# Batch 0's k loaded in rows of nine tokens and turned on TensorE, its scores by pairs of heads, decay folded into q, one MLP block's second part spread over output steps, the last output tile in halves

## The chip, the cores and the metric

The kernel runs on one core of a Trainium2 chip. The metric is the device time of one execution in microseconds (us). The core has five engines that run their own instruction lists and wait for each other by semaphores: TensorE (PE, with its weight loads PEld), VectorE (DVE), ScalarE (ACT), GpSimd (POOL) and SyncE (SP). SP, ACT and POOL also issue DMAs. Matrix products land in PSUM, eight banks of 128 x 512 fp32; everything else lies in SBUF.

## The reference

Eight batches of eight heads, 576 tokens, 64 features each. First a retention layer (attention without softmax, with a decay mask), then an MLP whose hidden layer is h times cos(h). The result is 4608 x 512 in fp32.

```python
scores = (q @ k.T) / sqrt(64)
gamma = 1 - 2 ** (-5 - head)
ret = scores * where(i >= j, gamma ** (i - j), 0)
x = (ret @ v)                    # heads side by side: 4608 x 512
h = x @ w_in                     # 512 x 2048
out = (h * cos(h)) @ w_out       # 2048 x 512
```

## The kernel before

**Retention by chunks.** The 576 tokens of a batch are cut into NCH = 5 chunks of 128 (the last 64); NP = 4 is the number of head pairs. The decay gamma^(i-j) is split: v is multiplied by gamma^-j (`vmul`, table WV, on POOL), and the result by gamma^i / 8 (table UP) when it leaves PSUM. For each chunk r of batch b: `scores` multiplies turned k by turned q (64-row operands, two banks, one for each head of a pair), and DVE multiplies both by a triangle (`mask`, tile rt); `rest` adds, into one bank (po), the state of the chunks before times q (weights sb) and the masked scores times v (rt, vb), then adds k times v into the state (bank st), which ACT copies to sb; at its end DVE multiplies po by UP into xt (L476).

**Layouts.** k and q are needed with features on partitions (tile kqt). From batch 2 on `prep` casts k and q on POOL into kqb, multiplies v, and a transposing DMA on SP's queue writes kqt. Batches 0 and 1 are turned on PE: k by `turn_k` (a product with the identity, one chunk at a time, from kqb), q by `turn_q` (from rows of nine tokens, 2304 contiguous bytes for each partition: a pair of heads fills 128 partitions and is turned by 18 small transposes). k and v of a chunk are loaded by `load`, 128 tokens by eight heads, in pieces of 256 bytes. Batch 0's q is loaded by `load_q0` in the nine-token rows and cast on DVE (`cast_q0`, L280).

**MLP by tiles.** The 4608 tokens are cut into NTB = 9 tiles of TB = 512, which straddle the batches. `mlp1(j, dt)` computes step dt of 16: four products (xt, win) into one of four mm banks, cosine on ACT (tile cb, L504), product with h on DVE (tile gt, L507). `mlp2(j, st, part)` adds a quarter of the 16 products that give the 128 output tokens st; after the last part ACT copies the bank to osb (L538), and ACT's queue stores it (L545). `bank` hands out the mm banks in turn and skips the ones that an unfinished output holds. The weights are loaded and cast by POOL's DMAs: `w_in_load` in five pieces (steps 0, 2, 4, 8, 12), `w_out_load` in four.

**Order.** `emit` writes the order out by hand. Each `self.s.op` goes into its engine's list at that place, and waits are derived from the `Buf` objects that it reads and writes. Before the first MLP step stand batch 0's chunks 0 to 3, with `spin` (idle products with the identity) between them; chunk 4 comes between steps 2 and 6 of the first tile (`turn_k`, `scores`, `rest`). Batch 1's first chunks stand between the output steps of tile 0, the others between the first parts (320 of 512 tokens) of tile 1's steps. The second parts (192 tokens) follow in a row, then tile 1's output steps with batch 2's chunks between. From then on each tile's output steps hold the next batch's chunks. On POOL the first w_in piece stands behind the casts of k's chunks 0 to 2 and two multiplications of v; the loads of batch 1 wait on SP for the landing of w_out's first piece.

L401 and L403 are the lines of all matmuls (in `group`: all but the last, and the last), L318 the casts, L308 `vmul`, L267 `load`, L296 `w_in_load`, L303 `w_out_load`, L365 and L381 the evictions of `turn_k` and `turn_q`, L428 `mask`, L471 the copies of the state.

## Time and profile before

| | us |
|---|---|
| median of 3 runs | 316.08 (315.33 to 316.46) |
| profiled execution | 315.09 |
| its span, first to last instruction | 313.3 |
| PE busy | 301.7 |
| PEld busy | 159.8 |
| DVE busy | 174.2 |
| ACT busy | 161.7 |
| POOL busy | 93.2 |

The granted clock of TensorE is 1.000 over the span, and DMA moves 48.85 MB. Matmuls overlap in the pipeline, so that a single one lasts longer (379 ns for 512 columns) than the step from one to the next (0.216 us). Rows of the timeline give the start, the duration, the engine, the line, the operation, output and inputs, and in brackets the idle time before it with what ended that. The matmuls of `spin` count as busy. An engine that is idle costs nothing unless PE waits for it in the end.

### The profile page before, as it was taken

How to read it: one execution, taken by the hardware profiler on the slowest of the kernel's cores; microseconds unless marked ns; L12 is line 12 of the kernel's file. 1: busy time of each engine (PE TensorE's matmuls, PEld its weight loads, DVE VectorE, ACT ScalarE, POOL GpSimd, SP SyncE). 2: the span in 40 equal slices, each digit the busy share in tenths (PEclk: the TensorE clock that was granted, in tenths of full speed). 3: DMA queues.
4: the chain of work that ended last, by engine and by line, in shares of the span. 5: the costliest groups of instructions: out<-in, count | busy, mean ns of one | idle time of the engine just before them, and what ended most of it. 6: DMA issues, size and time to landing. Idle time of an engine off the chain costs nothing.

```text
span 313.3 us, 6427 instructions
## 1 busy us (share of the span) xinstructions
PE 301.7 (96%) x2519; PEld 159.8 (51%) x2552; DVE 174.2 (56%) x301; ACT 161.7 (52%) x290; POOL 93.2 (30%) x128
## 2 busy tenths in 40 slices
PE   7979999999999999999999999999999999999996
PEld 6754455666554455445545554455445554444442
DVE  3567624788427852685458554865577448405700
ACT  7566525784347533762377236723573347317711
POOL 2693027444455434553535434110000000000000
DMA  7999999999999999999999999940001000120021
GB/s 211 214 180 207 200 220 231 260 192 187 233 252 170 239 216 249 224 221 231 233 231 202 237 245 212 137 86 36 33 0 69 36 33 0 51 85 1 15 82 73
DMA packets 142815, 48.85 MB, mean 156 GB/s; under 512 B 132545, under 2 KB 137665, under 8 KB 142785
## 3 DMA queue, kind: packets, MB, share of 16 engines
q1 hardware_dynamic: 132320, 34.22, 61.2%
q0 software_dynamic: 5280, 4.78, 9.4%
q10 hardware_dynamic: 5184, 9.44, 8.7%
q8 instruction: 20, 0.33, 0.5%
q14 instruction: 11, 0.08, 0.1%
HBM read 36.70 MB, written 9.44 MB: 147 GB/s over the span
## 4 chain that ended last, share of the span: by engine, by line
PE 90%; DMA 3%; issue 2%; ACT 2%; DVE 2%; SPq 1%; POOL 1%; DVEq 0%
PE mm L401 60%; PE mm L403 20%; PE po L401 6%; DMA vn<-in_v_dram 3%; PE sc L401 2%; PE st L401 1%; ACT cb L504 1%; DVE rt L428 1%; SPq L276 1%; DVE gt L507 0%; SPq L267 0%; DVE xt L476 0%; ACT osb L538 0%; ACT kqt L365 0%; POOL vb L308 0%
## 5 line engine op out<-in xcount | busy, mean ns | idle before, releaser
L507 DVE TENSOR_TENSOR gt<-mm,cb 128x512 bf16<-128x512 f32 (+2 forms) x160 | 101.2, 637 | 60.7 <-ACT cb L504 58.1
L401 PE MATMUL mm<-xt,win 128*128 128x512 bf16 (+2 forms) x471 | 116.7, 358 | 0.8 <-DVE xt L476 0.3
L504 ACT ACTIVATE cb<-mm,c_pih 128x512 bf16<-128x512 f32 (+2 forms) x160 | 101.9, 645 | 27.6 <-PE mm L403 26.8
L401 PE MATMUL mm<-wout,gt 128*128 128x512 bf16 x408 | 111.7, 379 | 3.2 <-issue 3.0
L401 PEld LDWEIGHTS mm<-xt,win 128*128 128x128 bf16 x480 | 44.6, 98 | 48.5 <-DVE gt L507 1.7
L401 PEld LDWEIGHTS mm<-wout,gt 128*128 128x128 bf16 x432 | 39.3, 98 | 44.4
L538 ACT ACTIVATE osb<-mm 128x512 f32<-128x512 f32 x36 | 21.5, 597 | 71.7 <-PE mm L403 71.7
L403 PE MATMUL mm<-xt,win 128*128 128x512 bf16 (+2 forms) x160 | 57.2, 358 | 0.3
L403 PE MATMUL mm<-wout,gt 128*128 128x512 bf16 x144 | 54.6, 379 | 0.2
L308 POOL TENSOR_TENSOR vb<-vn,wv 128x512 bf16<-128x512 f32 (+1 forms) x40 | 41.7, 1043 | 35.8 <-DMA vn<-in_v_dram 29.6
L476 DVE TENSOR_TENSOR xt<-po,up 128x512 bf16<-128x512 f32 (+1 forms) x39 | 24.7, 634 | 45.7 <-PE po L403 45.7
L471 ACT ACTIVATE sb<-st 64x256 bf16<-64x256 f32 x64 | 24.1, 377 | 35.6 <-PE st L403 34.7
L318 POOL CAST kqb<-kn 128x512 bf16<-128x512 f32 (+1 forms) x40 | 24.4, 611 | 59.1 <-DMA kn<-in_k_dram 51.1
L428 DVE TENSOR_TENSOR rt<-sc,mk 128x512 bf16<-128x512 f32 (+1 forms) x54 | 30.5, 600 | 4.8 <-PE sc L403 4.8
L403 PEld LDWEIGHTS mm<-xt,win 128*128 128x128 bf16 x160 | 15.7, 98 | 15.7
L318 POOL CAST kqb<-qn 128x512 bf16<-128x512 f32 (+1 forms) x30 | 18.4, 615 | 16.1 <-DMA qn<-in_q_dram 16.1
L403 PEld LDWEIGHTS mm<-wout,gt 128*128 128x128 bf16 x144 | 14.1, 98 | 17.0
L428 DVE TENSOR_TENSOR rt<-mm,mk 128x512 bf16<-128x512 f32 x26 | 16.6, 682 | 0.1
L401 PE MATMUL po<-rt,vb 128*64 128x128 bf16 (+1 forms) x273 | 15.2, 220 | 0.0
L401 PEld LDWEIGHTS po<-kqt,sb 128*128 128x128 bf16 x124 | 8.6, 98 | 7.8 <-DVE rt L428 1.5
L401 PEld LDWEIGHTS po<-rt,vb 128*64 128x64 bf16 (+1 forms) x273 | 9.3, 108 | 5.9 <-DVE rt L428 2.1
L401 PE MATMUL po<-kqt,sb 128*128 128x128 bf16 (+1 forms) x124 | 11.2, 213 | 0.5 <-POOL vb L308 0.2
(88 smaller groups left out, 147.5 us busy)
## 6 DMA issues: line engine op xcount, KB each, us to landing
out_dram<-osb ACTq DMA_DIRECT2D x36, 256.0 KB, 3.6
kn<-in_k_dram SPq DMA_DIRECT2D x32, 256.0 KB, 4.6
vn<-in_v_dram SPq DMA_DIRECT2D x32, 256.0 KB, 5.4
qn<-in_q_dram SPq DMA_DIRECT2D x24, 256.0 KB, 4.8
wout<-in_moe_w_out_dram POOLq DMA_DIRECT2D x4, 512.0 KB, 14.0
win<-in_moe_w_in_dram POOLq DMA_DIRECT2D x3, 512.0 KB, 7.5
qn<-in_q_dram SPq DMA_DIRECT2D x4, 288.0 KB, 4.7
kn<-in_k_dram SPq DMA_DIRECT2D x8, 128.0 KB, 3.6
```

The costliest lines, as they stand in the source:

```text
L276: s.dma("sp", f"q0_{c}", lambda e: e.dma_start(dst, src), writes=[self.bQN[c]])
L308: self.s.op(eng, lambda e: e.tensor_tensor(bass.AP(self.VB[i][r], 0, v3), self.staged("v", r, v3[1:]), bass.AP(self.WV, r * H_, [[NCH * H_ ...
L318: self.s.op(eng, lambda e: e.tensor_copy(o, f), reads=[self.bST32[x][r]], writes=[bt[i][r]])
L401: self.nc.tensor.matmul(o, a, b, **kw)
L403: return s.done("pe", self.nc.tensor.matmul(o, a, b, **kw), reads, writes)
L428: self.s.op("dve", lambda e: e.tensor_tensor(bass.AP(self.RT[k][hp], 0, p3), bass.AP(sc[0], 0, p3), bass.AP(self.MK, 0, [[CH, ck], [0, NP] ...
L471: s.op("act", lambda e: e.activation(bass.AP(self.SB[r % 2], 64 * hp * 512 + 64 * hp, [[512, 64], [128, NP], [1, D_]]), bass.AP(self.ST, 6 ...
L476: s.op("dve", lambda e: e.tensor_tensor(bass.AP(self.XT, t0, [[NP * XR, 128], [XR, NP], [1, ck]]), bass.AP(po, 0, [[512, 128], [CH, NP], [ ...
L504: s.op("act", lambda e: e.activation(co, mo, AF.Sin, bias=self.C_PIH.ap(), scale=1.0), reads=[bm, self.bC], writes=[bcb])
L507: s.op("dve", lambda e: e.tensor_tensor(bass.AP(g, dt * TB + o, [[16 * TB, 128], [1, n]]), mo, co, ALU.mult), reads=[bm, bcb], writes=[bg])
L538: s.op("act", lambda e: e.activation(o.ap(), m.ap(), AF.Copy), reads=[bm], writes=[bo])
```

## The change

What it does, in the order of the kernel:

- Batch 0's k is loaded in the nine-token rows, as q is (`load0`, eight loads alternating k and q by head pair), ahead of v's chunks 0 to 3. All eight are cast on POOL (`cast0`); k's rows use a part of the second gt tile that is free then. PE turns both (`turn0`), q's eviction multiplies by the decay, and `back0` turns k back into the token layout (kqb) that the state needs. All 576 tokens of k are turned, so the turning of chunk 4 falls away.
- Batch 0's scores run by pairs of heads over chunks 0 to 3 at once (`scores0`), their masked results lie in the gt tile too. `rest` is cut into `sums` and `state`; batch 0 runs three states, four sums in a row (evicted by ACT and DVE by turns), and the fourth state. There are three sb tiles.
- The factor gamma^i / 8 goes from the result into q: `qmul` on POOL in place of q's cast from batch 2 on (table UPN), and a multiplication by DVE in the evictions of `turn_q` and `turn0`. The result leaves PSUM by a plain copy.
- POOL's list: eight casts, v 0, w_in 0, v 1, v 2, w_in 1, v 3, w_in 2 to 4, w_out. v's chunk 4 and batch 1 are loaded once w_in's last piece has landed. ACT loads its table for the cosine before the turning.
- Chunk 4 of batch 0 goes from the first tile's MLP steps to its output steps 2 and 4; batch 1's first chunks move by a step each, and k's chunk 2 is turned in an mm bank.
- The second parts of tile 1's steps run two by two ahead of output steps 0 to 7 of that tile; batch 2's chunks stand at steps 2, 5, 8, 11 and 14. Each gt step has two `Buf` objects, one for either part, so that the first output tokens wait for the first part only.
- `mlp2` skips the bank that it has just finished when that bank would be next.
- The last 128 output tokens are computed in two halves of 256 columns, the first copied by DVE and stored from SP, the second copied by ACT and stored from ACT (`last`).

```diff
+SP1 = 3 * 64 + CH
...
+    def consts_n(self):
+        s = self.s
+        s.op("act", lambda e: e.activation(self.WV.ap(), self.LW.ap(), AF.Exp, scale=-1.0),
+             reads=[self.bLW], writes=[self.bWV])
+        s.op("act", lambda e: e.activation(self.UPN.ap(), self.LW.ap(), AF.Exp,
+                                           bias=self.C_LN8.ap(), scale=1.0),
+             reads=[self.bLW, self.bC], writes=[self.bUPN])
...
+    def load0(self, x, c):
         n = 9 * D_
-        self.s.op("dve", lambda e: e.tensor_copy(
-            bass.AP(self.QX[0], c * n, [[NP * n, 128], [1, n]]),
-            bass.AP(self.QN, c * n, [[NCH * DM, 128], [1, n]])),
-            reads=[self.bQN[c]] + self.bST32["q"], writes=[self.bQ0[c]])
+        dst = bass.AP(self.XN[x], c * n, [[NCH * DM, 128], [1, n]])
+        src = bass.AP(self.src[x], 2 * c * S_ * D_, [[n, 128], [1, n]])
+        self.s.dma("sp", f"{x}0_{c}", lambda e: e.dma_start(dst, src), writes=[self.bN0[x][c]])
...
+    def cast0(self, x, c):
+        n = 9 * D_
+        more = [] if x == "q" else [b for i in range(2) for b in self.bGT[1][2 * NP + 2 * c + i]]
+        self.s.op("pool", lambda e: e.tensor_copy(
+            self.rows0(x, c, 128, [0, [1, n]]),
+            bass.AP(self.XN[x], c * n, [[NCH * DM, 128], [1, n]])),
+            reads=[self.bN0[x][c]] + self.bST32[x], writes=[self.bX0[x][c]] + more)
...
+    def qmul(self, eng, b, r):
+        i = b % 2
+        self.mul(eng, "q", r, self.KQB[i], 2 * DM * r + DM, NCH * 2 * DM, self.UPN, self.bUPN, self.bQB[i][r])
...
-        for x in "kq":
-            self.cast("pool", x, b, r)
+        self.cast("pool", b, r)
+        self.qmul("pool", b, r)
         self.vmul("pool", b, r)
...
+    def turn9(self, m, rows, reads, bm):
...
         m2 = m.ap().bitcast(BF16)
-        self.group([(m2[64 * hp:64 * hp + 64, 64 * t:64 * t + 64],
-                     bass.AP(self.QX[i], 64 * hp * NP * n + c * n + t * D_, [[NP * n, 64], [1, D_]]),
+        self.group([(m2[64 * hp:64 * hp + 64, 64 * t:64 * t + 64], rows(hp, t),
                      bass.AP(self.ID, 64 * hp * 128 + 64 * hp, [[128, 64], [1, 64]]),
                      dict(start=True, stop=True, is_transpose=True))
...
+    def turn_q(self, b, c, bank):
+        s, i, n = self.s, b % 2, 9 * D_
+        m, bm = bank
...
+        done = s.op("dve", lambda e: e.tensor_tensor(o, f, self.up9(c), ALU.mult),
+                    reads=[bm, self.bUP], writes=[Buf()])
...
+    def turn0(self, x, c, bank, eng):
+        s, (m, bm) = self.s, bank
+        f = self.turn9(m, lambda hp, t: self.rows0(x, c, 64, [t * D_, [1, D_]], hp),
+                       [self.bX0[x][c]], bm)
...
+        if x == "q":
+            fn = lambda e: e.tensor_tensor(o, f, self.up9(c), ALU.mult)
+        elif eng == "dve":
+            fn = lambda e: e.tensor_copy(o, f)
+        else:
+            fn = lambda e: e.activation(o, f, AF.Copy)
+        done = s.op(eng, fn, reads=[bm] + [self.bUP] * (x == "q"), writes=[self.bT0[x][c]])
...
+    def back0(self, c, bank):
+        s, (m, bm) = self.s, bank
+        n = NCH - 1
+        t = self.group([(bass.AP(m, r * CH, [[512, 128], [1, 128]]),
+                         bass.AP(self.KQT[0], c * S_ + r * CH, [[TP, 128], [1, CH]]), self.ID.ap(),
+                         dict(start=r == 0, stop=r == n - 1)) for r in range(n)],
+                       [self.bT0["k"][c], self.bID], [bm])
+        o = bass.AP(self.KQB[0], c * 128, [[NCH * 2 * DM, 128], [2 * DM, n], [1, 128]])
+        f = bass.AP(m, 0, [[512, 128], [CH, n], [1, 128]])
+        done = s.op("act", lambda e: e.activation(o, f, AF.Copy), reads=[bm], writes=[Buf()])
...
+    def scores0(self, c, sc):
+        s, n = self.s, NCH - 1
+        mms = []
+        for r in range(n):
+            for hp in range(2):
+                base = 64 * hp * TP + c * S_ + CH * r
+                mms.append((
+                    bass.AP(sc[hp][0], r * CH, [[512, 128], [1, CH]]),
+                    bass.AP(self.KQT[0], base, [[TP, 64], [1, CH]]),
+                    bass.AP(self.KQT[0], TQ + base, [[TP, 64], [1, CH]]),
+                    dict(start=r == 0, stop=r == n - 1)))
+        t = self.group(mms, [self.bT0["k"][c], self.bT0["q"][c]], [sc[0][1], sc[1][1]])
...
+        for hp in range(2):
+            s.op("dve", lambda e: e.tensor_tensor(
+                bass.AP(self.GT[1], (2 * c + hp) * TB, [[16 * TB, 128], [CH, n], [1, CH]]),
+                bass.AP(sc[hp][0], 0, p3),
+                bass.AP(self.MK, 0, [[CH, 128], [0, n], [1, CH]]), ALU.mult),
+                reads=[sc[hp][1], self.bMK], writes=list(self.bR0[2 * c + hp]))
...
+    def rest(self, b, r, po=None, eng="dve"):
+        done = self.sums(b, r, po, eng)
+        if r < NCH - 1:
+            self.state(b, r)
+        done()
...
+    def sums(self, b, r, po=None, eng="dve"):
...
+        t0 = (b * S_ + q0) % XR
+        o = bass.AP(self.XT, t0, [[NP * XR, 128], [XR, NP], [1, ck]])
+        f = bass.AP(po, 0, [[512, 128], [CH, NP], [1, ck]])
+        fn = (lambda e: e.activation(o, f, AF.Copy)) if eng == "act" else (lambda e: e.tensor_copy(o, f))
+        return lambda: s.op(eng, fn, reads=[bpo], writes=self.bXT[t0 // GR:(t0 + ck) // GR])
...
+    def state(self, b, r):
...
+            s.op("act", lambda e: e.activation(
+                bass.AP(self.SB[r % 3], 64 * hp * 512 + 64 * hp, [[512, 64], [128, NP], [1, D_]]),
+                bass.AP(self.ST, 64 * hp * 512, [[512, 64], [D_, NP], [1, D_]]), AF.Copy),
+                reads=[self.bST], writes=[self.bSB[r % 3]] if hp else [Buf()])
...
         del self.open[st]
+        if self.n_mm % 4 == i:
+            self.n_mm += 1
...
+    def last(self, j, st):
+        s, g, n = self.s, self.GT[j % 2], DM // 2
+        i = self.n_osb % self.NOSB
+        for half in range(2):
+            m, bm = self.bank()
+            self.group([(m[:, 0:n],
+                         bass.AP(g, c * TB + 128 * st, [[16 * TB, 128], [1, 128]]),
+                         bass.AP(self.WOUT, c * DM + n * half, [[16 * DM, 128], [1, n]]),
+                         dict(start=c == 0, stop=c == 15)) for c in range(16)],
+                       [bg[1] for bg in self.bGT[j % 2]] + self.bWOUT, [bm])
+            o, f = self.OSB[i][:, n * half:n * half + n], m[:, 0:n]
+            b = Buf()
+            b.w, b.r = list(self.bOSB[i].w), list(self.bOSB[i].r)
+            if half:
+                s.op("act", lambda e: e.activation(o, f, AF.Copy), reads=[bm], writes=[b])
+            else:
+                s.op("dve", lambda e: e.tensor_copy(o, f), reads=[bm], writes=[b])
+            dst = bass.AP(self.out, (TB * j + 128 * st) * DM + n * half, [[DM, 128], [1, n]])
+            s.dma(("sp", "act")[half], f"o_{half}", lambda e: e.dma_start(dst, o), reads=[b])
...
-        self.load("k", 0, 0)
-        self.load_q0()
-        for x, r in (("v", 0), ("k", 1), ("v", 1), ("k", 2), ("k", 3), ("v", 2), ("v", 3),
-                     ("k", 4), ("v", 4)):
-            self.load(x, 0, r)
+        for c in range(NP):
+            for x in "kq":
+                self.load0(x, c)
+        for r in range(NCH - 1):
+            self.load("v", 0, r)
         self.consts_a()
-        for c in range(3):
+        for c in range(NP):
             self.consts_b(c)
-        for r in range(2):
-            self.casts(0, r)
-        self.cast("pool", "k", 0, 2)
+        self.consts_n()
+        s.op("act", lambda e: e.activation(self.JUNK.ap(), self.C_PIH.ap(), AF.Sin), reads=[self.bC])
+        for c in range(NP):
+            for x in "kq":
+                self.cast0(x, c)
+        self.vmul("pool", 0, 0)
         self.w_in_load(0)
-        self.cast("pool", "k", 0, 3)
+        self.vmul("pool", 0, 1)
+        self.vmul("pool", 0, 2)
         self.w_in_load(1)
-        for r in (2, 3):
-            self.vmul("pool", 0, r)
-            self.w_in_load(r)
-        self.w_in_load(4)
-        self.casts(0, 4)
+        self.vmul("pool", 0, 3)
+        for i in range(2, len(WI) - 1):
+            w = self.w_in_load(i)
...
+        self.spin(30, st)
+        for c in range(NP):
+            self.turn0("k", c, mm[c % 2], "act" if c else "dve")
+            if c:
+                self.back0(c - 1, mm[(c - 1) % 2])
+            else:
+                self.spin(4, st)
+            self.turn0("q", c, mm[2], "dve")
+            self.spin(4, st)
+            if c:
+                self.scores0(c - 1, sc[(c - 1) % 2])
+        self.back0(3, mm[1])
+        self.spin(8, mm[0])
+        self.state(0, 0)
+        self.scores0(3, sc[1])
+        self.spin(4, mm[0])
+        self.state(0, 1)
+        self.spin(14, mm[2])
+        self.state(0, 2)
+        self.spin(14, mm[2])
+        for r, bank in enumerate((mm[0], mm[1], mm[2], sc[0][0])):
+            self.sums(0, r, bank, ("act", "dve")[r % 2])()
+        self.state(0, 3)
+        self.spin(6, po)
+        self.n_mm = 3
+        self.load("v", 0, NCH - 1, after=[w])
+        self.vmul("pool", 0, NCH - 1)
+        for r in range(NCH):
+            for x in "kv":
+                self.load(x, 1, r, after=[w])
         for r in range(NCH):
...
         for dt in range(16):
             self.mlp1(0, dt)
-            if dt == 2:
-                self.turn_k(0, 4)
...
         self.fetch(2)
-        for r in range(NCH):
-            self.feed(2, r, 3 if r == NCH - 1 else 1)
+        for r in range(NCH - 1):
+            self.feed(2, r)
...
+            if n == 2:
+                self.scores(0, 4)
+            if n == 4:
+                self.rest(0, 4)
+                self.feed(2, NCH - 1, 3)
             if n == 7:
                 for c in range(NP):
-                    self.turn_q(1, c, ("act", "dve")[c % 2], spare[c])
-            if n in (8, 10):
-                self.turn_k(1, n // 2 - 4, spare[0])
-            if n in (9, 12):
-                self.scores(1, n // 3 - 3)
-            if n == 13:
+                    self.turn_q(1, c, spare[c])
+            if n in (9, 11):
+                self.turn_k(1, n // 11, spare[0])
+            if n in (10, 13):
+                self.scores(1, n // 13)
+            if n == 14:
                 self.rest(1, 0)
-            if n == 14:
-                self.turn_k(1, 2, spare[0])
+                self.turn_k(1, 2, self.bank())
...
-        for dt in range(16):
-            self.mlp1(1, dt, n, TB - n)
...
-                if n == 0 and b <= B_:
+                if j == 1:
+                    if n == 2:
+                        self.rest(1, NCH - 1)
+                        self.scores(2, 0)
+                    elif n % 3 == 2:
+                        self.stage(2, n // 3 - 1)
+                elif n == 0 and b <= B_:
                     self.rest(b - 1, NCH - 1)
-                if b < B_:
...
+                if j == 1 and n < 8:
+                    for dt in (2 * n, 2 * n + 1):
+                        self.mlp1(1, dt, SP1, TB - SP1)
+                if (j, n // 4) != (NTB - 1, 3):
+                    self.mlp2(j, n // 4, n % 4)
         self.flush()
+        self.last(NTB - 1, TB // 128 - 1)
```

## The prediction

> **What bounds the kernel now.** The shares of busy time came first, then the chain of work that ended last, then the timeline stage by stage. From the page, the shares and the chain by engine:
>
> ```profile
> PE 301.7 (96%) x2519; PEld 159.8 (51%) x2552; DVE 174.2 (56%) x301; ACT 161.7 (52%) x290; POOL 93.2 (30%) x128
> PE 90%; DMA 3%; issue 2%; ACT 2%; DVE 2%; SPq 1%; POOL 1%; DVEq 0%
> ```
>
> TensorE (PE) is the bound nearly everywhere, so an edit counts only where PE waits or does needless work. Busy time per stretch (sum of the stretch, then PE, PEld, DVE, ACT, POOL, clock, DMA share, GB/s) says where:
>
> ```profile
> 15.00:20.80 5.80, 4.46 (x96) 3.36 (x91) 4.46 (x7) 4.37 (x10) 5.76 (x8) 1.00 1.17 176
> 20.80:35.90 15.10, 14.56 (x86) 6.70 (x89) 10.43 (x17) 10.52 (x17) 5.14 (x7) 1.00 1.23 205
> 67.40:74.60 7.20, 6.97 (x90) 5.41 (x90) 6.53 (x20) 6.50 (x18) 3.24 (x5) 1.00 1.28 191
> 139.30:171.60 32.30, 31.77 (x256) 16.20 (x255) 19.50 (x32) 16.19 (x29) 14.65 (x19) 1.00 1.13 223
> ```
>
> A steady tile (last row) lacks only 0.5 us of PE: nothing to win there. Before 20.8 us PE mostly spins while POOL is full (5.76 of 5.80), and from 67.4 us on PE, DVE and ACT are all near full. The timeline around the start of the first MLP (start, duration, engine, instruction):
>
> ```profile
> 14.03 0.92 POOL L296 DMA_DIRECT2D win<-in_moe_w_in_dram  x1
> 17.27 0.79 POOL L296 DMA_DIRECT2D win<-in_moe_w_in_dram  x1
> 18.08 1.06 POOL L308 TENSOR_TENSOR vb<-vn,wv 128x512 bf16<-128x512 f32 x1
> 20.80 0.33 PEld L401 LDWEIGHTS mm<-xt,win 128*128 128x128 bf16 x3 [0.28 <-DVE xt L476]
> 35.88 0.53 PEld L401 LDWEIGHTS mm<-wout,gt 128*128 128x128 bf16 x3
> 53.63 0.23 PEld L401 LDWEIGHTS po<-kqt,sb 128*128 128x128 bf16 x4 [0.58 <-ACT kqt L365]
> ```
>
> The first MLP matmul starts at 20.80, the first tile's second half at 35.88; PE waits 0.58 at 53.63. All sums are made against the profiled execution: 315.09 us, of which 313.3 are span and 1.8 lie around it. The median of the runs shown, 316.08, is 1.0 higher, so I carry the difference over to the median.
>
> **Part 1: the way to the first MLP matmul (20.80 now).** k's five loads in 256-byte pieces go; k and q come in eight loads of 295 KB in rows of 2304 bytes, v after them. The rate by the microsecond, while q's long rows ran and while v's and k's short ones ran:
>
> ```profile
> 6.00:7.00 1.00, 0.41 (x11) 0.23 (x9) 0.46 (x1) 0.48 (x1) 0.00 (x0) 1.00 1.00 360
> 12.00:13.00 1.00, 1.00 (x30) 0.85 (x29) 0.47 (x1) 0.65 (x3) 0.56 (x1) 1.00 0.96 181
> ```
>
> The casts of q's second, third and fourth load, each waiting for it, start at 6.42, 7.30 and 8.14, so long-row loads land 0.85 apart; six loads of k and v that land from 9.35 to 16.5 took 1.19 each. The first load landed at 4.1. So with 0.9 a load q's last lands at 4.1 + 7 x 0.9 = 10.4, and v's at 11.6, 12.8, 14.0, 15.2. SP issues the eight in 8 x 0.45, so its queue is no limit.
> POOL now does eight casts of 128x576. Its 128x512 cast is 0.611, so 0.69 each, faster than the rows land; DVE's four casts of 0.46 go. Then by rows: v0's multiplication (1.04) 11.6 to 12.7, w_in 0 issued (0.92) to 13.6, v1 to 14.6, v2 to 15.7, w_in 1 (0.8) to 16.5, v3 to 17.5, w_in 2.
> After v2 PE has: state 2 (0.28), 14 spins (0.80), four sums (0.30 + 3 x 0.55), drain 0.2, eviction 0.69, in all 4.0 with the hand-overs. That is 19.7; with v's late by what w_in 0 takes from them, 19.9. **Gain 0.9**, bounds 1.5 (rows at 0.8) and 0 (w_in 0 and slow rows together). The rest is covered: ACT's seven evictions of 0.65 and 0.60 end near 13, DVE's eight masks of 0.65 and four decayed evictions of q (nearest, the same size copied at 0.75) near 16; both are over when the sums start at about 16.8. Without that cover each microsecond late is one lost. Two more of v's terms leave this path: chunk 4 of v loads after w_in.
>
> **Part 2: first tile, first half (15.08 now).** 16 steps of 0.864 are 13.82; the rest is batch 0's fifth chunk: turning k (0.31), scores 0.33, sums with a stall 0.8. The turning disappears, the rest moves. But w_in 2 is issued at 17.5 instead of 17.27 and MLP step 4 wants it at 19.9 + 3.5 = 23.4. From the DMA issues w_in's pieces took 5.9, 6.0, 6.8, 7.5 and 9.3 from issue to landing. With the 6.8 of the same piece it lands at 24.3, a stall of 0.9; but in the old run that piece stood behind w_in 1 (landed 21.5, then 2.6 for each next megabyte) and short rows, which are through by 16 now. With the lowest row, 5.9, the stall is 0. I take 0.4: **gain 0.85**, bounds 1.26 and 0.3.
> The Trainium skill, "DMA: Bandwidth & Descriptors", section "Anatomy of one DMA — SWDGE (gpsimd) path", fits such a transfer as 2.0 us plus bytes over 436 GB/s: 4.4 us for this piece, and so no stall. The rows of this case, 5.9 to 9.3 with other traffic beside, are longer, and I go by them.
>
> **Part 3: first tile, second half (19.28 from 35.88 to 55.16).** It takes in the scores (0.33) and sums (0.65 without the stall) of the fifth chunk: loss 1.0. The turn of k's third chunk takes a free bank in place of PO, so the 0.58 wait at 53.63 mostly goes: gain 0.5. q of batch 1 is evicted by DVE alone, 4 x 0.75 = 3.0 instead of 1.5 in parallel; scores come 4.2 us after the first turn, so this is covered, with 0.6 to spare. Batch 1's loads start when w_in 4 has landed (about 28.5) and no longer at w_out 0 (31.8), so w_out has company earlier. The pieces in between landed 2.6 us apart alone and 3.3 with company; the third is needed at about 41.9 and comes near 40.8. **Loss 0.5**, bounds 0.3 and 1.5.
>
> **Part 4: block 1's second part.** Now 16 steps of 192 columns run in a row, DVE behind:
>
> ```profile
> 69.03 0.42 PE L401 MATMUL mm<-xt,win 128*128 128x192 bf16 x3 [0.22 <-DVE gt L507]
> 68.50 6.39 DVE L507 TENSOR_TENSOR gt<-mm,cb 128x320 bf16<-128x320 f32 x17
> ```
>
> They take 67.34 to 73.81 = 6.47, and PE needs 16 x 0.333 = 5.33. Spread two by two over eight output steps DVE has 1.5 us for 0.8: gain 1.14. Against it, batch 2's scores come singly: two more changes to the 64-row shape, 0.16 to 0.2 each: loss 0.35. **Gain 0.8**, bounds 1.1 and 0.
>
> **Part 5: decay in q.** 30 POOL casts of 0.615 become multiplications, by the row of v 1.04: +13 us on an engine that is 30% busy and waits for loads in every batch. DVE's multiplication of xt becomes a copy (0.69 against 0.68): nothing. What hides it is POOL's idle time, 17.6 of 32.3 us in the steady tile. If that were gone it would cost 0.43 per chunk. **0**, bounds -0.3 and +0.5 over all tiles.
>
> **Part 6: the tail.** The last eviction and store issue of the kernel:
>
> ```profile
> 310.36 0.60 ACT L538 ACTIVATE osb<-mm 128x512 f32<-128x512 f32 x1 [2.86 <-PE mm L403]
> 310.98 0.34 ACTq L545 DMA_DIRECT2D out_dram<-osb  x1
> ```
>
> Half as wide, the ACT copy costs 0.38 (its 128x256 row): 0.22 less. The store took 2.0 from issue to landing; half of it takes between 1.0 and 2.0, and I take 1.8. PE needs 32 x 0.108 in place of 16 x 0.216. **Gain 0.4**, bounds 0.2 and 1.2.
>
> **Sum:** -0.9 - 0.85 + 0.5 - 0.8 + 0 - 0.4 = -2.45. Profiled 312.6; median 316.08 - 2.45 = **313.6**.
>
> **Rivals.**
> *w_in comes too late* (PE waits for weights in place of attention). For it: w_in 1 and 2 stand behind multiplications that wait for v, and w_in 0 itself slows v. Against: less short-row traffic. If v's multiplications come 0.8 later and w_in 2 takes the 7.5 of the piece after it, it lands at 18.3 + 7.5 = 25.8 and holds step 4; the twelve steps left end at 36.2, 0.3 behind the old 35.88 instead of 1.75 ahead. That is 2.05 over my sum: 315.65, no change that can be told (315.0 with 6.8).
> *Slower: the long rows do not run fast.* One mechanism: eight rows at 220 GB/s (the short rows' 1.19 per 262 KB), 1.34 each. For it: one window of that time (4 to 5 us) moved only 180 GB/s, and q's first and second cast start 1.6 apart (4.80, 6.42). Against: 316 and 360 in the next two. Then the last lands at 13.5, v2 is ready at 18.8, the first MLP matmul at 22.8 and w_in 2 (issued 20.6, plus 6.8) stalls step 4 by 1.1. That is 2.9 + 0.7 over my sum: 317.2. The case decides for slower once the first MLP matmul comes after 19.9 + 2.45 = 22.3.
> *More than forecast:* rows at 0.8, no stall, a store halved in time: 1.5 + 1.26 - 0.3 + 1.1 + 1.0 = 4.6, 311.5.
> *The spreading does not take effect* (the stalls go into the output steps, for want of banks): part 4 gives -0.35, and the time is 314.8. It stays on the faster side, within the forecast's own case.
>
> **How the numbers follow.** About 0.3% (0.95 us) is what a measurement of this kernel can tell from no change. Forecast, 312.0 to 315.1 with both its outcomes of part 4: 0.60. More than forecast: 0.10. w_in late: 0.14. Slow rows: 0.16. Faster 0.70, same 0.14, slower 0.16. The range reaches up into the slow-row case and down to the large gain: 310.9 to 316.9.
>
> **What would show it.** In the changed profile: POOL casts under 1 us apart up to about 11; the first MLP matmul at 19.5 to 20.5; at most one wait for w_in, at step 4, under 1 us; no DVE wait inside 192-column steps; the last store issue 0.4 before the old distance from the last matmul. A first MLP matmul after 21, or waits for w_in or w_out above 1 us, makes the prediction wrong.

## The result, and the profile after

The changed kernel takes 314.54 us (median of 16 runs, 313.75 to 316.1). The kernel before, run beside it, takes 316.26 (16 runs, 315.33 to 317.89): a ratio of 0.9949, interval 0.9935 to 0.9963, so 1.7 us faster, as forecast in sign and nearly in size (313.6, range 310.9 to 316.9). The profiled execution of the changed kernel lasts 314.30 us with a span of 312.6; that of before lasted 315.09 with 313.3. The two traces thus lie only 0.7 apart, and only these 0.7 can be followed in them one by one. Two executions of the experiments below that took far longer than the rest, one of tail_whole (519.96) and one of the kernel before (791.13), are left out of all medians.

From the page of the changed kernel, busy time by engine and the chain of work that ended last by engine:

```profile
PE 301.5 (96%) x2578; PEld 162.2 (52%) x2614; DVE 176.8 (57%) x311; ACT 160.3 (51%) x283; POOL 107.8 (34%) x131
PE 94%; ACT 3%; issue 2%; POOL 0%; DVE 0%; ACTq 0%
```

PE now holds 94% of the chain instead of 90%, and DMA (3% before) has left it: no wait for a load ends on the path any more. POOL has 14.6 us more work, most of it the decay in q. Busy time by stretch (length, then PE, PEld, DVE, ACT, POOL, clock, DMA share, GB/s), the same stages as before:

```profile
6.00:7.00 1.00, 0.58 (x22) 0.41 (x20) 0.12 (x1) 1.00 (x4) 0.85 (x2) 1.00 1.05 376
12.00:13.00 1.00, 1.00 (x30) 0.75 (x25) 1.00 (x3) 0.90 (x2) 0.98 (x3) 1.00 1.26 223
15.00:22.30 7.30, 6.41 (x124) 4.94 (x124) 3.33 (x6) 4.52 (x11) 7.28 (x11) 1.00 0.90 121
22.30:35.90 13.60, 13.53 (x62) 6.16 (x63) 9.68 (x14) 10.27 (x15) 0.73 (x1) 1.00 1.21 196
139.30:171.60 32.30, 31.77 (x255) 16.24 (x256) 19.59 (x31) 16.26 (x28) 16.94 (x20) 1.00 1.18 221
```

The long rows do run fast (376 GB/s in the seventh microsecond), the steady tile is the same to the hundredth of PE (31.77 of 32.30), and the first tile's first half is nothing but its products (13.53 of 13.60). But the stretch ahead of it ends at 22.3, not at 20.8. The stage marks, all from the timelines of PE:

| us | before | after | difference | forecast |
|---|---|---|---|---|
| first MLP matmul | 21.03 | 22.32 | +1.29 | -0.9 |
| first tile, first half | 15.06 | 13.59 | -1.47 | -0.85 |
| first tile, second half | 19.08 | 19.63 | +0.55 | +0.5 |
| second tile, 320-column parts | 12.30 | 12.30 | 0 | 0 |
| from the 192-column parts to the third tile | 24.94 | 24.27 | -0.67 | -0.8 |
| third tile to the last matmul's end | 217.91 | 217.96 | +0.05 | 0 |
| last matmul's end to the end | 2.98 | 2.53 | -0.45 | -0.4 |
| sum | 313.3 | 312.6 | -0.7 | -2.45 |

(The mark 21.03 of before is the first product on record; the 20.80 in the prediction was its weight load. In both traces the record of the very first of its four products is missing, so both marks are some 0.2 late and both first halves 0.2 short. By the weight loads the start moved from 20.80 to 22.09, by the same 1.29.) Two parts came as forecast, and the start, meant to win 1.75 in the first two rows, wins 0.18 and then loses 0.55. Where it went shows in PE's timeline of the changed kernel (start, duration, line, output and inputs; in brackets the idle time and what ended it):

```profile
9.80 0.44 PE L491 MATMUL mm<-ident,gt 64*64 64x64 bf16 x17 [0.98 <-ACT kqb L449]
13.78 0.23 PE L493 MATMUL st<-ident 128*128 128x128 bf16 x1 [0.71 <-issue]
15.35 0.31 PE L491 MATMUL st<-vb,kqb 128*64 128x64 bf16 x7 [0.24 <-ACT kqb L449]
16.54 0.31 PE L491 MATMUL st<-vb,kqb 128*64 128x64 bf16 x7 [0.22 <-ACT sb L585]
17.73 0.31 PE L491 MATMUL st<-vb,kqb 128*64 128x64 bf16 x7
22.32 0.59 PE L491 MATMUL mm<-xt,win 128*128 128x512 bf16 x2 [0.45 <-DVE xt L566]
```

and in those of ACT and POOL:

```profile
2.33 1.28 ACT L266 ACT_TABLE_LOAD   x1 [2.33 <-POOL ig L264]
3.63 3.15 ACT L266 ACTIVATE up<-ig,c_ln,lng 128x576 f32<-128x576 f32 x4
7.14 1.28 ACT L694 ACT_TABLE_LOAD   x1
8.54 0.63 ACT L434 ACTIVATE kqt<-mm 128x576 bf16<-128x576 bf16 x1
14.70 0.60 ACT L449 ACTIVATE kqb<-mm 128x512 bf16<-128x512 f32 x1 [1.46 <-PE mm L493]
```

```profile
9.78 0.67 POOL L302 CAST qx<-qn 128x576 bf16<-128x576 f32 x1
14.26 1.04 POOL L339 TENSOR_TENSOR vb<-vn,wv 128x512 bf16<-128x512 f32 x1 [0.27 <-DMA vn<-in_v_dram]
```

POOL and the loads are even earlier than forecast (last cast at 9.78 against 10.4, v2 ready at 15.30 against 15.7). The third state, which needs v2, starts at 17.73 all the same. What holds it is PE and ACT between them. ACT's exponential table waits for POOL's `ig` until 2.33, so its first eviction of k comes at 8.54, and PE waits for it (0.98 at 9.80). PE then stands for 0.71 before 13.78 with no releaser in the profile ("issue"). So the last turning back of k is evicted by 15.30, the first state starts at 15.35, and the states follow 1.19 apart, each after ACT's copy of the one before. The forecast counted only the third. The four sums then come 0.68 apart (18.86, 19.54, 20.21, 20.89 in PE's timeline), where it counted 0.55.

The Trainium skill, "ScalarE: Activation LUTs", section "What ACT_TABLE_LOAD costs", prices a change of tables at 1283 ns plus a drain of about 1380 ns, 2.66 us in all. The load agrees (1.28); the drain is not to be seen here, for the load at 7.14 stands 0.02 behind the activation before it, and the next begins 0.01 after it. By the page's sum the first eviction would have come at about 9.9, as an estimate; it came at 8.54.

### The profile page after: what moved, and what is told of

The parts are those of the page before. It is cut to its first block, busy times and chain, and to the rows that moved or that the text cites. A ratio compares the mean times of both kernels' runs of the same rounds, so it can differ in the third digit from the quotient of the medians.

```text
span 312.6 us, 6548 instructions
## 1 busy us (share of the span) xinstructions
PE 301.5 (96%) x2578; PEld 162.2 (52%) x2614; DVE 176.8 (57%) x311; ACT 160.3 (51%) x283; POOL 107.8 (34%) x131
## 4 chain that ended last, share of the span: by engine, by line
PE 94%; ACT 3%; issue 2%; POOL 0%; DVE 0%; ACTq 0%
PE mm L491 63%; PE mm L493 21%; PE po L491 6%; PE sc L491 3%; PE st L491 2%; ACT up L266 1%; ACT L694 0%; ACT L266 0%; ACT kqb L449 0%; ACT sb L585 0%; DVE xt L566 0%; POOL ig L264 0%; ACT kqt L434 0%; PE st L493 0%; ACT osb L668 0%
## 5 line engine op out<-in xcount | busy, mean ns | idle before, releaser
L491 PE MATMUL mm<-wout,gt 128*128 128x512 bf16 (+1 forms) x424 | 111.6, 372 | 3.0 <-issue 2.7
L491 PEld LDWEIGHTS mm<-xt,win 128*128 128x128 bf16 x480 | 45.5, 98 | 49.0 <-DVE gt L615 0.6
L491 PEld LDWEIGHTS mm<-wout,gt 128*128 128x128 bf16 x450 | 40.9, 98 | 42.0 <-DVE gt L615 0.2
L493 PE MATMUL mm<-wout,gt 128*128 128x512 bf16 (+1 forms) x142 | 53.6, 377 | 0.3
L649 ACT ACTIVATE osb<-mm 128x512 f32<-128x512 f32 x35 | 20.9, 597 | 62.8 <-PE mm L493 62.8
L566 DVE CAST xt<-po 128x512 bf16<-128x512 f32 (+1 forms) x36 | 22.7, 630 | 41.8 <-PE po L493 41.8
L339 POOL TENSOR_TENSOR kqb<-qn,upn 128x512 bf16<-128x512 f32 (+1 forms) x30 | 31.2, 1041 | 17.7 <-DMA qn<-in_q_dram 17.5
L350 POOL CAST kqb<-kn 128x512 bf16<-128x512 f32 (+1 forms) x35 | 21.3, 608 | 45.7 <-DMA kn<-in_k_dram 42.4
L518 DVE TENSOR_TENSOR rt<-sc,mk 128x512 bf16<-128x512 f32 (+1 forms) x52 | 29.2, 596 | 4.7 <-PE sc L493 4.7
L493 PEld LDWEIGHTS mm<-xt,win 128*128 128x128 bf16 x160 | 15.7, 98 | 15.7
L493 PEld LDWEIGHTS mm<-wout,gt 128*128 128x128 bf16 x142 | 13.9, 98 | 16.6
L491 PE MATMUL po<-rt,vb 128*64 128x128 bf16 (+1 forms) x252 | 14.0, 220 | 0.0
L518 DVE TENSOR_TENSOR rt<-mm,mk 128x512 bf16<-128x512 f32 x20 | 12.8, 678 | 0.0
L491 PE MATMUL po<-kqt,sb 128*128 128x128 bf16 (+1 forms) x116 | 10.4, 212 | 0.0
```

The costliest lines, as they stand in the source:

```text
L339: self.s.op(eng, lambda e: e.tensor_tensor(bass.AP(t, o, [[pitch, ck], [D_, H_], [1, D_]]), self.staged(x, r, [[D_, H_], [1, D_]]), bass.A ...
L350: fn = (lambda e: e.activation(o, f, AF.Copy)) if eng == "act" else (lambda e: e.tensor_copy(o, f))
L491: self.nc.tensor.matmul(o, a, b, **kw)
L493: return s.done("pe", self.nc.tensor.matmul(o, a, b, **kw), reads, writes)
L518: self.s.op("dve", lambda e: e.tensor_tensor(bass.AP(self.RT[k][hp], 0, p3), bass.AP(sc[0], 0, p3), bass.AP(self.MK, 0, [[CH, ck], [0, NP] ...
L566: fn = (lambda e: e.activation(o, f, AF.Copy)) if eng == "act" else (lambda e: e.tensor_copy(o, f))
```

## The experiments

The kernel before was run beside each group of experiments: 316.06 (12 runs) beside before_again, old_start, exp_early and no_spin; 315.51 (30 runs) beside no_idle_loop, exp_early_no_spin, no_spread and decay_out; 315.8 (17 runs) beside spin_44, spin_20, best and tail_whole. These medians and the 316.26 beside the changed kernel differ by up to 0.75, so kernels of different groups are compared by their ratios to the kernel before.

**before_again** is the kernel before, unchanged, profiled once more.

> The kernel before, unchanged, for a second profile. Its first profile (315.09 us, span 313.3) lies below all 16 timed runs (315.33 to 317.89). If that profile was a lucky one, a second shows a span near 314.5, and the extra 1.2 us lies ahead of the first MLP matmul (weights' first product at 21.03 in the first profile) or in the first tile, where loads are waited for. If the stretch after the first tile is what varies, the first MLP matmul stays at 21.0 and the extra shows up later.

316.41 us, span 314.7, so 1.4 longer than the first profile. 1.34 of it lies ahead of the second half of the first tile: the first MLP matmul at 21.64, and the first half 15.79 long, with one wait in PE's timeline:

```profile
25.93 0.81 PE L401 MATMUL mm<-xt,win 128*128 128x512 bf16 x3 [0.56 <-DMA win<-in_moe_w_in_dram]
```

All other stages agree to 0.06. The kernel before varies in its start, where loads land sooner or later, and the profile on which the prediction was built was one of its quickest executions: 315.09 lies below all 16 runs timed beside the changed kernel.

**old_start** is the kernel before with only the last two parts of the change, the spreading and the halved last tile (among the edits not shown, batch 2's chunks move and `mlp2` skips the bank just finished, as in the change).

```diff
-        for dt in range(16):
-            self.mlp1(1, dt, n, TB - n)
...
+                if j == 1 and n < 8:
+                    for dt in (2 * n, 2 * n + 1):
+                        self.mlp1(1, dt, SP1, TB - SP1)
...
+        self.last(NTB - 1, TB // 128 - 1)
```

> The kernel before with only two parts of the change: tile 1's second part spread over output steps, and the last output tile in halves; the way to the first MLP matmul, the fifth chunk and the decay are as before. Theory: these two parts are worth what the two profiles show, 0.67 and 0.45 to 0.7, so 1.1 to 1.4 below before (ratio 0.9957 to 0.9965). Rival: the new start is what gains, since the medians differ by 1.7 and the profiles by 0.8; then this one is at most 0.5 faster than before.

314.25 us (6 runs), ratio 0.9937, interval 0.9915 to 0.9959: as fast as the whole change (0.9949, 0.9935 to 0.9963). In its profile the first MLP matmul stands at 21.51,

```profile
21.51 0.59 PE L402 MATMUL mm<-xt,win 128*128 128x512 bf16 x2 [0.91 <-DMA win<-in_moe_w_in_dram]
```

with a wait for w_in that the new start doesn't have; from the 192-column parts to the third tile it takes 24.29, and the span is 312.8. So the new start (rows of nine tokens, turning there and back, scores by pairs, decay in q, the fifth chunk moved) gives nothing that can be measured: by the ratios the two kernels lie 0.4 apart, in old_start's favour and well within the intervals. The gain is the other two parts.

**no_spread** undoes the spreading in the changed kernel, **tail_whole** the halved last tile.

```diff
+        for dt in range(16):
+            self.mlp1(1, dt, SP1, TB - SP1)
...
-                if j == 1 and n < 8:
-                    for dt in (2 * n, 2 * n + 1):
-                        self.mlp1(1, dt, SP1, TB - SP1)
```

> The changed kernel with tile 1's second parts in a row again and batch 2's chunks where they were before. Theory: it loses what the two profiles show for this part, from the first 192-column product to the next tile's first product 24.94 against 24.27: 0.6 to 0.8 slower than the changed kernel. Rival: the later start of the first MLP matmul, not this, is what decides; then within 0.3 of it.

```diff
-                if (j, n // 4) != (NTB - 1, 3):
-                    self.mlp2(j, n // 4, n % 4)
-        self.flush()
-        self.last(NTB - 1, TB // 128 - 1)
+                self.mlp2(j, n // 4, n % 4)
+        self.flush()
```

> Changed kernel with its last output step undone: one step of 512 columns and one store, as before the change. If part 6 gains 0.4 as forecast: last product to the end of the span 2.98 instead of 2.53, 0.45 above the changed kernel, 315.0. Rival (the halves' second handover and store cost what they save): 314.5, and the same distance to the end.

no_spread: 315.07, ratio 0.9995 (0.9969 to 1.0021), and the stage in question takes 24.93 as before, against 24.27. tail_whole: 315.38 (11 runs), ratio 0.999 (0.9975 to 1.0006), and 3.03 from the last matmul's end to the end, against 2.53. Each alone brings the time back to that of the kernel before, within the intervals. By the stages the two are worth 0.67 and 0.5, some 1.1 of the timed gain of 1.7 (1.2 to 2.1 by the interval); where the rest comes from, no pair of profiles here shows. Some executions also have a lower mean granted clock and take longer: three of the eleven of tail_whole and three of the ten of no_spread, but two of the sixteen of the changed kernel. The timeline of tail_whole and that of the changed kernel show what the halves save:

```profile
311.70 0.60 ACT L649 ACTIVATE osb<-mm 128x512 f32<-128x512 f32 x1 [2.86 <-PE mm L493]
312.33 0.34 ACTq L677 DMA_DIRECT2D out_dram<-osb  x1
```

```profile
310.11 0.38 ACT L668 ACTIVATE osb<-mm 128x256 f32<-128x256 f32 x1 [2.90 <-PE mm L493]
310.52 0.34 ACTq L672 DMA_DIRECT2D out_dram<-osb  x1
```

0.22 is the narrower copy; the rest of the 0.5 is the smaller store, whose landing takes 1.7.

**decay_out** takes the decay out of q again: q is cast, and the multiplication by UP goes back to where the result leaves PSUM.

```diff
-        self.qmul("pool", b, r)
+        self.s.op("pool", lambda e: e.tensor_copy(
...
+        return lambda: s.op("dve", lambda e: e.tensor_tensor(o, f, up, ALU.mult),
```

> The changed kernel with gamma^i / 8 multiplied into the result again, as before: q is cast on POOL, q's evictions copy, and all evictions of the sums are multiplications on VectorE (two of batch 0's four no longer on ScalarE). Theory: nothing, within 0.3 of the changed kernel; POOL's 13 us lie in its idle time. Rival: the longer POOL work delays the transposing DMAs; then this is up to 0.5 faster. Rival: two evictions by ScalarE shorten the way to the first MLP matmul; then this is up to 0.5 slower.

314.11, ratio 0.9956 (0.9931 to 0.998), span 312.4: no difference from the changed kernel that can be told. POOL is busy for 95.2 us there and for 107.8 in the changed kernel; the longer multiplications are hidden, as forecast.

**The start.** Four kernels take its suspects away, alone and together. **exp_early** loads the exponential table by an activation that waits for nothing but `ip`; **no_spin** leaves out the 14 spins behind the third state; **exp_early_no_spin** is both; **no_idle_loop** leaves out the 20 spins in the turning loop.

```diff
+        s.op("act", lambda e: e.activation(self.JUNK2.ap(), bass.AP(self.IP, 0, [[NCH, 128], [1, 1]]), AF.Exp,
+                                           scale=-1.0), reads=[self.bIP])
```

> The changed kernel with one added ScalarE instruction: a 1-column exponential of an index that is ready at 1.0, at the head of ScalarE's list, so that the table for the exponential loads at 0.8 in place of 2.33. Theory: the first MLP matmul (22.32 in the changed kernel's profile, 19.9 forecast) is held by ScalarE, whose evictions start at 8.5, behind two table loads and four exponentials; 1.3 earlier there makes the first MLP matmul 1.0 to 1.6 earlier and the time 1.0 to 1.6 shorter. Rival 1: the chain is held by v's multiplications or by the products that idle between the states; then the first MLP matmul stays within 0.3. Rival 2: w_in's pieces (the third landed at 23.35) hold step 4 of the first tile; then the matmul moves but a wait of the same size opens at step 4 or later and the time stays.

```diff
         self.state(0, 2)
-        self.spin(14, mm[2])
```

> The changed kernel without the 14 idle products between the third state and the four sums (they take 0.85). Theory: the four sums need only the masks (done at 17.3) and the states before, so they start 0.85 earlier, and with them the first MLP matmul and the end: 0.6 to 0.85 shorter. Rival: the fourth sum waits for the third state's copy (18.87) or w_in's third piece holds step 4; then less than 0.3.

> The changed kernel with the early exponential table and without the 14 idle products ahead of the four sums. Theory: the early table alone gave nothing in time because PE's standstill at the 222nd matmul grew by what ScalarE saved (1.38 against 0.71); taking the idle products away gave 0.7 to 0.8 in the timed runs. Together they give what the second gives, 0.7 to 0.9 under the changed kernel. If the two add up instead, 1.5 to 2.

```diff
-            else:
-                self.spin(4, st)
             self.turn0("q", c, mm[2], "dve")
-            self.spin(4, st)
```

> The changed kernel without the 20 idle products between the turnings of batch 0's k and q. In the three profiles of the new start so far PE stands 0.71, 1.38 and 1.53 with no releaser at one and the same instruction, the 222nd matmul, whatever the time. Theory (PE runs out of fetched instructions there): the standstill goes to the 222nd matmul again, which is now the last of the 8 idle products behind the last turning back, after batch 0's third scores. Since 20 of the products before it are real ones that wait for data, it shrinks by up to 0.3, and the time stays within 0.5 of the changed kernel. Rival (something at that place in the order, the fourth turning of q, holds PE): the standstill stays between the fourth turning of q and the third scores, or goes with the idle products.

exp_early: 314.62 (0.9961, 0.9934 to 0.9987), nothing gained. Its timeline shows why: ACT is 1.3 earlier, and PE gives it back in the standstill (the idle time of 0.71 with no releaser that was seen above before 13.78).

```profile
0.81 1.28 ACT L232 ACT_TABLE_LOAD   x1 [0.81 <-PEq L835]
7.27 0.63 ACT L437 ACTIVATE kqt<-mm 128x576 bf16<-128x576 bf16 x1
13.58 0.23 PE L496 MATMUL st<-ident 128*128 128x128 bf16 x1 [1.38 <-issue]
```

PE comes to the same matmul 0.87 earlier (12.20 against 13.07), and goes on at almost the same time. no_spin: 313.74 (0.9927, 0.9901 to 0.9952), by the ratios 0.7 better than the changed kernel, near the length of the spins, but the intervals overlap, so the gain is not shown; nor does its profile show it, since there the standstill was 1.53 and the first MLP matmul came at 23.21. exp_early_no_spin: 314.16 (0.9962, 0.9944 to 0.998), by its ratio no faster than the changed kernel, though its profile has the first MLP matmul at 21.29 and a span of 311.8, the shortest of all; its timed runs scatter from 313.08 to 316.11. no_idle_loop: 314.53 (0.9962, 0.995 to 0.9975), no standstill at all, and no gain either. Its stretches (columns as above) show the price:

```profile
6.00:8.00 2.00, 0.80 (x22) 0.58 (x22) 0.81 (x2) 1.98 (x5) 1.41 (x3) 1.00 0.99 355
8.00:10.00 2.00, 1.41 (x34) 1.14 (x36) 1.25 (x2) 1.65 (x4) 1.84 (x3) 0.53 1.16 339
10.00:12.00 2.00, 2.00 (x48) 1.60 (x44) 1.00 (x3) 1.14 (x2) 1.29 (x3) 0.50 1.24 222
12.00:14.00 2.00, 2.00 (x48) 1.55 (x46) 1.65 (x3) 1.14 (x2) 1.98 (x3) 0.50 0.81 158
```

PE is busy for 0.80 of two microseconds, and for the next six it gets half its clock. That is no accident of this one execution: ten of the twelve timed ones have a mean granted clock of 0.989 or 0.995, two of sixteen in the changed kernel. The idle products are there for that. What share of idle time it takes is not shown: tail_whole is busy for 0.93 of the same two microseconds and keeps its clock in the next six. The theory that the standstill belongs to a count of products had it moved into the next row of spins; it vanished, with PE late to that place. That settled nothing.

**What the standstill is.** Two more kernels change only the first row of spins, far ahead of it, in idle time: **spin_44** has 14 products more, **spin_20** has ten fewer.

```diff
-        self.spin(30, st)
+        self.spin(44, st)
```

> The first row of spins has 44 products instead of 30; nothing else is changed. It ends about 1.0 to 1.5 us later, which PE's waits of 0.42, 0.23 and 0.98 before the third turning of q take in. Theory (PE's standstill with no releaser belongs to the number of products issued, as when its next instructions are not there yet): it still precedes the 222nd product, which is now 14 products earlier in the program, the 8th of the 18 that turn q's last row block; the group of 17 is split there. Rival (the standstill belongs to what is computed there, a wait that the profile does not name): it stays before the last of the four spins behind that turning. First MLP product 22.0 to 23.0 by either.

> The first row of spins has 20 products instead of 30. Theory of the number of products: the 222nd is now ten products later in the program, behind the scores of the third pair of heads, the second of the four that turn k's last block back; the standstill is there, and shorter than 0.71 or gone, for PE comes there some 0.4 later. Rival: it stays before the last of the four spins behind q's last turning. First MLP product 21.9 to 22.3 by the theory, 22.3 by the rival.

PE's timelines, of spin_44 and then of spin_20:

```profile
12.47 0.31 PE L491 MATMUL mm<-ident,qx 64*64 64x64 bf16 x7
13.44 0.34 PE L491 MATMUL mm<-ident,qx 64*64 64x64 bf16 x10 [0.66 <-issue]
```

```profile
13.88 0.23 PE L491 MATMUL mm<-ident,kqt 128*128 128x128 bf16 x1
14.38 0.29 PE L491 MATMUL mm<-ident,kqt 128*128 128x128 bf16 x2 [0.27 <-issue]
```

The standstill moved by exactly 14 and by exactly 10 products, into the middle of a turning that waits for nothing. It precedes the 222nd product of the program, whatever is computed there. The rival, a wait at that place that the profile doesn't name, is out. The page of each kernel lists two DMA queues of the kind "instruction", q8 with 20 packets and q14 with ten or eleven; for which engine they work, no view says. In the changed kernel, a stretch of the DMA view of 0.12 us holds the first packet of q8:

```profile
DMA packets 101, 0.04 MB, mean 341 GB/s; under 512 B 100, under 2 KB 100, under 8 KB 100
q8 instruction: 1, 0.02, 66.6%
```

Found in the same way in the others (the last column is the weight load, as the prediction counts, because the first product is not on record in all of these traces):

| us | first packet starts | PE goes on | first MLP weight load |
|---|---|---|---|
| spin_44 | 10.62 to 10.75 | 13.44 | 22.22 |
| exp_early | 10.75 to 10.88 | 13.58 | 21.90 |
| no_spread | 10.75 to 10.88 | 13.65 | 21.96 |
| decay_out | 10.88 to 11.0 | 13.66 | 21.97 |
| exp_early_no_spin | 10.88 to 11.0 | 13.76 | 21.06 |
| after | 11.0 to 11.12 | 13.78 | 22.09 |
| spin_20 | 11.5 to 11.62 | 14.38 | 22.14 |
| no_spin | 11.88 to 12.0 | 14.60 | 22.98 |
| tail_whole | 11.88 to 12.0 | 14.61 | 23.70 |
| before | 9.88 to 10.0 | no standstill | 20.80 |

PE goes on 2.7 to 2.8 after the packet starts, nine times out of nine, while the packet itself varies by 1.2 from execution to execution. In the kernel before, 2.75 after its packet is 12.7, and PE reaches its 222nd product at about 14.9: nothing to wait for. That PE lacks instructions there is thus supported by count and time, not shown outright: no row names the wait. What starts the packet, and why at such different times, stays open. Where the program between the standstill and the MLP is in essence that of the changed kernel, and the clock full, the first MLP weight load follows 8.31 to 8.32 after PE goes on (after, exp_early, no_spread, decay_out): in these kernels the standstill's end sets the start of the MLP.

**best** puts together what the profiles promise most from: the early table, no 14 spins, 20 first spins.

> Changed kernel with ACT's exponential table loaded by an early exponential that waits for nothing, without the 14 spins behind the third state, and with 20 first spins instead of 30. Forecast from exp_early_no_spin (first MLP product at 21.29, 314.16) and a standstill moved ten products on: first MLP product at 20.9 to 21.3, 313.8. Theory that the start is set by PE's standstill and the chain of states: 0.5 to 1.0 below the changed kernel's 314.54. Rival that the start's later end is given back by waits for weights in the first tile: 314.5, with a wait for the third piece of w_in at step 4.

313.49 us (6 runs, 313.27 to 314.26), ratio 0.993, interval 0.9918 to 0.9942: 2.3 below the kernel before, the lowest median of all, and by the ratios about 0.6 below the changed kernel; but the intervals overlap, so this last step is not shown. There is no standstill in its profile, and no wait for weights in its first tile. That profile, of the slowest of its runs, has the first MLP matmul only at 21.88 (forecast 20.9 to 21.3), for its small products ran slow until 14 us: the same 17 transposes took 0.69 at 11.13 and 0.48 at 13.99, both at a granted clock of 1.00 in the profile's stretches. Rows of best, and then one of spin_20:

```profile
11.13 0.69 PE L494 MATMUL mm<-ident,qx 64*64 64x64 bf16 x17
13.99 0.48 PE L494 MATMUL mm<-ident,qx 64*64 64x64 bf16 x17
21.88 0.82 PE L494 MATMUL mm<-xt,win 128*128 128x512 bf16 x3 [0.23 <-DVE xt L569]
```

```profile
9.99 0.68 PE L491 MATMUL mm<-ident,gt 64*64 64x64 bf16 x17
```

The row at 13.99 is q's last turning, which began at 11.46 in exp_early. In best the first packet of instructions starts at 10.62 to 10.75, and PE reaches its 222nd product only after 15, more than 4 later, so there is nothing to wait for. The shorter first row is itself a suspect for the slow products: in both kernels with 20 first spins these transposes still take 0.68 at 10 us, while every kernel with 30 or 44 has them at 0.44 to 0.48 from 8 us on, save no_idle_loop with its halved clock. No run tests this, nor best with 30 first spins.

## Why the prediction was right, and where it was wrong

**Part 1** failed, by 2.2 us. Its terms for loads and casts held: long rows 0.75 to 0.8 apart from the third on (0.9 taken), a cast 0.67 (0.69), w_in issued at 11.99, 15.24 and 17.05. The failed step is "After v2 PE has: state 2 (0.28), 14 spins (0.80), four sums (0.30 + 3 x 0.55), drain 0.2, eviction 0.69". It took v as the chain that ends last. In its place the runs showed a chain over PE and ACT: the standstill until 13.78, ACT's last eviction at 15.30 (the prediction had them "end near 13"), three states 1.19 apart and not one of 0.28. From the third state on 4.6 us pass where 4.0 were counted, 0.3 of it in the sums. The prediction's own sign of being wrong, a first MLP matmul after 21, was met: it came at 22.09 by the weight load, the mark that the prediction uses.

**Part 2** was right in its mechanism and too small: 1.47 against 0.85, and above its bound of 1.26. Two terms were mis-sized. One is the stall of 0.4 for the third piece of w_in: there was none. The piece took 6.3 from its issue (6.8 and 5.9 were the bounds) and landed at 23.35; step 4 came only at 25.55, since the MLP started late. With the forecast's start at 19.9 it would have come at 23.4, just in time. The transfer and step 4 in the changed kernel, and the first product of the second half in the kernel before:

```profile
win<-in_moe_w_in_dram POOLq DMA_DIRECT2D x1, 512.0 KB, 6.3
25.55 0.81 PE L491 MATMUL mm<-xt,win 128*128 128x512 bf16 x3
```

```profile
36.09 0.81 PE L401 MATMUL mm<-wout,gt 128*128 128x512 bf16 x3
```

The other 0.2 lies in the marks. The 15.08 runs from a weight load after idle time (20.80), whose product follows within 0.01 where it is on record (21.87 and 21.88 in best), to a weight load that runs 0.2 ahead of its product (35.88 and 36.09). From product to product it is 15.3, so the fifth chunk took 1.46 and not 1.26. The fit of the Trainium skill, "DMA: Bandwidth & Descriptors", section "Anatomy of one DMA — SWDGE (gpsimd) path", gives 4.4 for this transfer, as an estimate; with the other traffic beside it, it was 6.3 here.

**Part 3** (0.55 lost, 0.5 forecast), **part 4** (0.67 won, 0.8 forecast), **part 5** (nothing) and **part 6** (0.45 or 0.5 won, 0.4 forecast) were right, each shown by undoing it or by its stage, except part 3, which was only read from the stage. In the spread 192-column steps PE never waits for DVE (once, for 0.23 at 68.89, an output step does); DVE now waits for ACT's cosine instead, off the path:

```profile
69.54 0.41 PE L491 MATMUL mm<-xt,win 128*128 128x192 bf16 x3
70.60 0.69 DVE L615 TENSOR_TENSOR gt<-mm,cb 128x192 bf16<-128x192 f32 x2 [0.73 <-ACT cb L612]
```

The last store's issue came only 0.2 nearer to the last matmul and not 0.4; the shorter landing made up the rest.

**The time** was nearly met because two errors offset each other in part. The parts add up to -0.7 in the traces and not to -2.45, 1.75 too much gain. But the prediction carried the distance of the profile before from its median, 1.0, over to the changed kernel. That distance was the luck of one quick execution; the changed kernel's profile lies only 0.24 below its median, and these 0.75 go the other way. What is left is 0.9. The range, 310.9 to 316.9, takes in the kernel before as well, so that a time inside it says little about the mechanism. The rival of slow rows, which was to decide from a first MLP matmul at 22.3, saw that mark nearly reached (22.09) by another mechanism: its rows of 1.34 did not occur, and the first tile gave 0.6 more than counted. "w_in comes too late" did not happen for the same reason as in part 2.

## What to carry to other kernels

When one chain of a prologue is shortened, write down the next two with their hand-overs: here v was made early, and a chain of three dependent states with ACT's copy in each, and a standstill of PE that looks like a lack of instructions, were as long. Small edits at places where PE alone sets the end (a burst of narrow steps that waits for one engine, the last copy and store) kept nearly all that they promised (0.67 of 0.8, and 0.45 of 0.4). And a sum made against one profile should use a second one of the same kernel, to see which stages vary by themselves.

## What the hardware showed that was not expected

PE can stand still with nothing to wait for: before its 222nd product here, for 0.27 to 1.53 us, until 2.7 to 2.8 after the first packet of a queue of instructions starts. The reading that fits count and time is that 220 short products packed into some 12 us run faster than their instructions come.

Such a standstill can go with a loss of clock. In tail_whole and no_spin, where it was 1.53 long, the granted clock of PE fell afterwards (to 0.50); behind 1.38 in exp_early and all shorter ones it stayed at 1.00. The stretches of tail_whole's profile:

```profile
14.00:16.00 2.00, 1.39 (x16) 1.10 (x17) 0.55 (x1) 0.01 (x1) 1.62 (x3) 0.67 1.09 143
16.00:18.00 2.00, 2.00 (x28) 1.52 (x26) 0.99 (x3) 1.34 (x3) 1.98 (x3) 0.50 0.36 40
```

The first MLP weight load comes 9.1 after PE goes on there, against 8.3, which adds to the scatter of the kernels with the new start.
